# Attention and Strassen's FFN1 on one core: a planner by due times, block 0's sums shared by VectorE and GpSimd, first maxima on TensorE, every other block backward

## The chip, the core and the metric

The kernel runs on one core of a Trainium2 chip. The metric is the device time of one execution in microseconds. TensorE (PE), VectorE (DVE), ScalarE (ACT), GpSimd (POOL) and SyncE (SP, which issues DMAs) each run their own instructions in the order in which the program lists them, and wait for one another by semaphores.

## What is computed

Linear attention over 8 batches, 8 heads, 576 positions of 64, and then a feed-forward network on the 4608 x 512 result. The weights are float64, the rest float32.

```python
q_s = softmax(q, over the 64 of a head)
k_s = softmax(k, over the 576 positions)      # needs a maximum over positions
kv  = einsum('bhsd,bhde...', k_s^T, v)        # 64 x 64 for each head
x   = (q_s @ kv), reshaped to 4608 x 512
h   = x @ w_in                                # 512 x 2048
g   = h * sigmoid(1.702 h)
out = g @ w_out                               # 2048 x 512
```

## The kernel before

**Blocks, pairs, steps.** The 4608 tokens are nine blocks of 512. FFN1 and FFN2 of a block take eight steps, one for each *pair* p of w_in's and w_out's column groups. A step has 15 slots. In it `ffn1` does Strassen's seven products (line 581), each as six matmuls of 256 columns, in two PSUM banks, Y and Z (`PROD`, line 561). VectorE's adds (line 594) and ScalarE's copies empty these banks, and the same bank is written again by the next product but one. `ffn2` (line 643) follows one step later in banks 0 to 3. The last step's sums are copied out (line 655) and stored.

**Splits.** A product is made of float32r halves: a value's rounded part h (a cast on ScalarE) and its remainder l = value - h (a subtraction: line 551 for x, 625 for g, 274 for w_in, 312 for w_out). Strassen's sums come before that: s1, s2, s3, s4 of x in `x_sums` (line 525; VectorE in block 0, GpSimd in the others), and four sums of w_in's parts (line 251, GpSimd) in the staging tile `st`.

**Weights.** w_in and w_out come as float64 and are turned into float32 on the chip while block 0 runs: `high` (line 238, ScalarE, on the upper words), `low` (242, VectorE, shifts the lower words), `narrow` (234 and 235, two VectorE instructions: the first joins the words, the second puts the sign back). `conv_wi` then makes the seven tiles `wa` (3) and `wb` (4) of a pair, and stores them to DRAM (`kept`, line 277). There are two buffers each of `wa` and `wb` (p % 2), so in blocks 1 to 8 `load_kept` (line 288) brings each pair back, by DMAs that GpSimd issues. The w_out tiles stay.

**Attention.** The attention of block t runs beside the FFN of block t - 1 (block 0's own at the start). Key batch b belongs to block t = b; I call it key block b. `k_max` has VectorE take maxima over the 4 positions of a partition (lines 382 to 384), and GpSimd the maximum over the 128 partitions, for each of four head pairs (`partition_all_reduce`, line 388). `k_sub` subtracts it (400, 403) and ScalarE takes exp (406). `q_soft` (460 to 470) does the same for q along a row, `q_tr` transposes q on PE (483), `kv_pairs` (437) and `x_pairs` (504) are the small matmuls. ScalarE needs one table for exp and one for gelu (597).

**The order.** Every operation is given to `Plan` with an engine, a cost, what it reads and writes, and a rank. `Plan.order` (line 47) plays the engines forward: whenever one is free it takes, of its ready operations, the one with the lowest rank. The order in which the operations began is the program's order on every engine. The costs are those of lines 24 and 99 to 108; a change of ScalarE's table costs 1.28 us there, one of GpSimd's programs nothing.

```python
def dve(n, psum=False):
    return 0.15 + n / 960
...
def pool(n):
    return 0.25 + n / 480
```

The functions that the change touches, and what calls them:

Of the kernel before, what the change touches and what calls it, by code (L numbers as in the profile page):

```python
# [18 lines left out]
class Plan:  # L19
# [4 lines left out]
    HOP, LAND, RATE, ISSUE, TABLE = 0.1, 1.8, 270e3, 0.5, 1.28  # L24
# [22 lines left out]
    def order(self):  # L47
        ops = self.ops
        left = [len(o[2]) for o in ops]
        users = [[] for _ in ops]  # L50
        for n, o in enumerate(ops):
            for d in o[2]:
                users[d].append(n)
        engines = sorted({o[0] for o in ops})
        free = dict.fromkeys(engines, 0.0)
        ready = {e: [] for e in engines}
        coming = []
        at = [0.0] * len(ops)
        for n, o in enumerate(ops):
            if not left[n]:  # L60
                heapq.heappush(ready[o[0]], (o[3], n))
        wire, table = 0.0, None
        began = []
        self.start = {}
        now = 0.0
        while len(began) < len(ops):
            while coming and coming[0][0] <= now:
                _, n = heapq.heappop(coming)
                heapq.heappush(ready[ops[n][0]], (ops[n][3], n))
            moved = False  # L70
            for e in engines:
                if free[e] > now or not ready[e]:
# [10 lines left out]
                self.start[n] = now  # L83
                moved = True
                for u in users[n]:
# [5 lines left out]
            if not moved:  # L91
                times = [f for e, f in free.items() if f > now and ready[e]]
                if coming:
                    times.append(coming[0][0])
                now = min(t for t in times if t > now) if any(t > now for t in times) else now
        return began


def dve(n, psum=False):
# [7 lines left out]
def pool(n):  # L107
    return 0.25 + n / 480
# [3 lines left out]
def efficient_attention_then_gelu_ffn(  # L112
# [54 lines left out]

    ident = sb("ident", [P, P])
# [9 lines left out]
    st = sb("st", [P, 7, 2 * P])  # L178
# [4 lines left out]
    mx = [sb(f"mx{i}", [P, 2, D]) for i in range(2)]  # L183
    m1 = sb("m1", [P, 2, 2, D])
    qm = [sb(f"qm{i}", [P, 2 * C]) for i in range(2)]
# [9 lines left out]
    first = sb("first", [P, D])  # L195
    nc.vector.memset(first, 0.0)
    nc.gpsimd.partition_all_reduce(first, first, P, bass_isa.ReduceOp.max)
# [5 lines left out]
    plan.add("POOL", 7.0, (), ("first",), -3000, lambda: None)  # L203
# [8 lines left out]
    def load_w(p, kind, rank):  # L212
        for jj in range(2):
# [12 lines left out]
            plan.add("SP", plan.ISSUE, (), (tag,), rank + 0.01 * jj, run, size=2 * DM * 4 * P)  # L226

    def words(raw):
        return raw.rearrange("p (f t) -> p f t", t=2)

    def narrow(f, w):
# [16 lines left out]
    ST_ = [("st", n) for n in range(7)]  # L248

    def sub(o, x, y):  # L250
        nc.gpsimd.tensor_tensor(out=st[:, o], in0=st[:, x], in1=st[:, y], op=ALU.subtract)

    def conv_wi(p, rank):
        i = p % 2
        for jj, at_ in enumerate((0, 5)):
            T, K = f"wo{p}{jj}", ST_[at_ : at_ + 2]
            f = flat(st[:, at_ : at_ + 2])
# [6 lines left out]
            plan.add("DVE", 1.36, (T, *K), K, rank, lambda f=f, w=w: narrow(f, w()))  # L264
# [477 lines left out]
```

## Time and profile before

| | us |
|---|---|
| median of 3 runs | 1035.72 (1033.41 to 1045.96) |
| the profiled execution | 1033.14 |
| its span in the profile | 1031.4 |
| PE busy | 865.9 (84%) |
| VectorE busy | 567.9 (55%) |
| ScalarE busy | 498.3 (48%) |
| GpSimd busy | 207.0 (20%) |

The span runs from the first to the last instruction of the program. "Idle before" in a row is how long the engine did nothing just before the instruction, with the event that ended it.  Granted clock 1.00 is 2.4 GHz for TensorE, 0.50 is 1.2 GHz.

### The profile page before, as it was taken

The page shows a single profiled execution, that of the slowest core. Times are in us where ns is not written, and L with a number is a line of the kernel's source. Part 1 is how long each engine was busy: PE and PEld are TensorE (multiplying, and loading weights), DVE is VectorE, ACT ScalarE, POOL GpSimd, SP SyncE. Part 2 cuts the span into 40 slices and gives each one's busy share as a digit, 9 for nine tenths or more (in the row PEclk, how much of TensorE's full clock was granted, in tenths as well). Part 3 has the DMA queues.
Part 4 walks back from the last instruction along what each step waited for, and adds up shares of the span by engine and source line. Part 5 has one row for each costly group of instructions (what it writes and reads, how often), then busy time and mean ns, then how long its engine had stood idle before and what let it go on. Part 6 is the DMA issues. An engine that isn't in the chain of part 4 may idle for free.

```text
span 1031.4 us, 15064 instructions
## 1 busy us (share of the span) xinstructions
PE 865.9 (84%) x5792; PEld 748.3 (73%) x5792; DVE 567.9 (55%) x1103; ACT 498.3 (48%) x861; POOL 207.0 (20%) x247
## 2 busy tenths in 40 slices
PE   3523873457689999999796999997999999999998
PEld 2322652346568898888686789886889889888887
DVE  7885994549677343453565653535553663235332
ACT  3552753347658343543555942526543742334322
POOL 1432332323232011120133021101311211021100
PEclk9675996669899999999998999998999999999999
DMA  9991842149565565466757655566476556447551
GB/s 256 277 328 46 246 147 91 49 152 253 177 171 177 184 215 171 136 235 202 209 152 208 205 179 173 182 229 177 131 235 204 173 173 219 150 143 237 164 181 42
DMA packets 126088, 187.64 MB, mean 182 GB/s; under 512 B 84544, under 2 KB 100928, under 8 KB 116800
## 3 DMA queue, kind: packets, MB, share of 16 engines
q0 software_dynamic: 18432, 117.45, 34.9%
q1 hardware_dynamic: 107584, 69.22, 23.0%
q8 instruction: 46, 0.75, 0.3%
q14 instruction: 26, 0.21, 0.1%
HBM read 162.53 MB, written 24.12 MB: 181 GB/s over the span
## 4 chain that ended last, share of the span: by engine, by line
PE 66%; DVE 14%; issue 7%; DMA 5%; ACT 2%; SPq 2%; POOL 2%; DVEq 0%; POOLq 0%; ACTq 0%
PE bank L643 32%; PE bank L581 30%; DMA qt<-in_q 2%; PE bank L504 2%; DVE gl L625 1%; DMA kt<-in_k 1%; PE bank L437 1%; PE bank L483 1%; DVE qt L461 1%; DVE xl L551 1%; SPq L368 1%; DVE kt L400 1%; DVE raw L242 1%; DMA vt<-in_v 1%; DVE g L594 1%
## 5 line engine op out<-in xcount | busy, mean ns | idle before, releaser
L643 PE MATMUL bank<-w,gh 128*128 128x512 f32 x1152 | 372.8, 405 | 34.8 <-ACT w L308 26.3
L581 PE MATMUL bank<-xh,wb 128*128 128x256 f32 x1152 | 257.0, 288 | 30.5 <-DVE tu L594 13.3
L643 PE MATMUL bank<-w,gl 128*128 128x512 f32 x576 | 230.4, 400 | 11.2 <-DVE gl L625 11.2
L581 PE MATMUL bank<-xh,wa 128*128 128x256 f32 x864 | 190.1, 294 | 56.0 <-POOL wa L274 20.7
L643 PEld LDWEIGHTS bank<-w,gh 128*128 128x128 f32 x1152 | 194.1, 193 | 57.3 <-ACT w L308 27.1
L581 PEld LDWEIGHTS bank<-xh,wb 128*128 128x128 f32 x1152 | 199.1, 192 | 49.1 <-DVE tu L594 15.7
L581 PEld LDWEIGHTS bank<-xh,wa 128*128 128x128 f32 x864 | 149.6, 197 | 71.4 <-POOL wa L274 21.9
L581 PE MATMUL bank<-xl,wb 128*128 128x256 f32 x576 | 164.6, 286 | 0.0
L597 ACT ACTIVATE g<-g 128x512 f32<-128x512 f32 (+1 forms) x144 | 75.5, 525 | 176.2 <-DVE g L594 171.4
L643 PEld LDWEIGHTS bank<-w,gl 128*128 128x128 f32 x576 | 110.6, 192 | 42.5 <-DVE gl L625 15.8
L625 DVE TENSOR_TENSOR gl<-g,gh 128x512 fp32r<-128x512 f32 x144 | 110.1, 772 | 28.2 <-ACT gh L622 27.9
L581 PE MATMUL bank<-xl,wa 128*128 128x256 f32 x432 | 125.4, 290 | 0.0
L581 PEld LDWEIGHTS bank<-xl,wb 128*128 128x128 f32 x576 | 110.4, 192 | 9.6
L594 DVE TENSOR_TENSOR tu<-bank,ta 128x256 f32<-128x256 f32 x72 | 30.4, 422 | 134.2 <-PE bank L581 134.2
L622 ACT CAST gh<-g 128x512 fp32r<-128x512 f32 x144 | 89.4, 621 | 4.5
L288 POOL DMA_DIRECT2D wb<-kb x64 | 35.4, 552 | 275.8 <-PE bank L581 275.8
L581 PEld LDWEIGHTS bank<-xl,wa 128*128 128x128 f32 x432 | 85.3, 197 | 5.0
L288 POOL DMA_DIRECT2D wa<-ka x64 | 35.2, 550 | 259.7 <-PE bank L581 242.6
L597 ACT ACTIVATE g<-bank 128x256 f32<-128x256 f32 x72 | 27.7, 385 | 71.0 <-PE bank L581 70.0
L400 DVE TENSOR_TENSOR kt<-kt,mx 128x512 f32<-128x512 f32 x32 | 24.9, 779 | 61.4 <-POOL mx L388 61.4
L594 DVE TENSOR_TENSOR g<-bank,ts 128x256 f32<-128x256 f32 x72 | 30.4, 422 | 46.3 <-PE bank L581 45.7
L594 DVE TENSOR_TENSOR g<-bank,ta 128x256 f32<-128x256 f32 x72 | 30.5, 423 | 46.0 <-PE bank L581 45.6
(76 smaller groups left out, 968.1 us busy)
## 6 DMA issues: line engine op xcount, KB each, us to landing
wb<-kb POOLq DMA_DIRECT2D x64, 1024.0 KB, 5.2
wa<-ka POOLq DMA_DIRECT2D x64, 768.0 KB, 4.7
out<-tmp SPq DMA_DIRECT2D x36, 256.0 KB, 4.2
kt<-in_k SPq DMA_DIRECT2D x32, 256.0 KB, 3.9
vt<-in_v SPq DMA_DIRECT2D x64, 128.0 KB, 4.1
raw<-in_moe_w_in SPq DMA_DIRECT2D x16, 512.0 KB, 8.7
raw<-in_moe_w_out SPq DMA_DIRECT2D x16, 512.0 KB, 4.8
kb<-wb SPq DMA_DIRECT2D x8, 1024.0 KB, 5.1
```

What stands on the lines that cost most here:

```text
L242: nc.vector.tensor_scalar(lo, lo, 29, None, ALU.logical_shift_right)
L288: nc.gpsimd.dma_start(out=tl.rearrange("p s n f -> p (s n f)"), in_=kept[p][u == "wb"])
L368: nc.sync.dma_start(out=qt[hp][p0:p1, :, o : o + m], in_=src.rearrange("h (p c) d -> p c h d", c=C))
L400: nc.vector.tensor_tensor(out=t, in0=t, in1=m.unsqueeze(2).broadcast_to([P, 2, CM, D]), op=ALU.subtract)
L437: nc.tensor.matmul(pk[r0 : r0 + D, m, :], lhs, rhs, start=c == 0, stop=c == CM, tile_position=(0, r0))
L504: nc.tensor.matmul(po[ro], kvn[b % 2][ri, hp, :], qx[ri], start=True, stop=True, tile_position=((a ^ odd) * D, a * D),)
L581: nc.tensor.matmul(ph[bk], tl[:, s, place, c * P : (c + 1) * P], x[:, c, :], start=opens and c == 0 and e == 0, stop=c == 1 and e == 2, sk ...
L594: return lambda: nc.vector.tensor_tensor(out=o, in0=ph[bk], in1=x, op=ALU.add)
L597: return lambda: nc.scalar.activation(o, x, AF.Gelu_apprx_sigmoid)
L622: vec("ACT", act(2 * n), half, (H,), slot, lambda c=c, gh=gh: nc.scalar.copy(gh, c))
L625: nc.vector.tensor_tensor(out=gl, in0=c, in1=gh.bitcast(F32), op=ALU.subtract)
L643: nc.tensor.matmul(bank[c], l, r, start=first_ and e == 0, stop=last and e == 2)
```

## The change

- **Due times.** `Plan.due` walks backward from the PE operations, which are laid end to end in rank order, and gives each operation the latest time at which it may begin. `Plan.forward` takes the ready operation with the earliest due time instead of the lowest rank. SP may be at most 6 us of transfer ahead of the wire. A change of GpSimd's program costs 7.0 us there now, and the DMA rate is 310 GB/s instead of 270.
- **Shared operations.** An operation of the kind `EITHER` goes to VectorE or GpSimd, whichever is free first. `sb_op` makes such an operation; its callers ask for it in block 0 and for the attention of block 1: the sums of w_in's parts, the remainders of `wa`, `wb`, w_out, x and g, `k_sub`, the subtraction and the scaling of `q_soft`, `x_sums`. Otherwise `sb_op` puts it on VectorE. So `x_sums` of blocks 2 to 8 moves from GpSimd to VectorE.
- **First maxima.** For key blocks 0 and 1 the maximum over partitions is a transpose on PE, a reduction on VectorE, a matmul of the broadcast column with the identity, and a copy on ScalarE. From key block 2 on it is the all-reduce, which reads the tokens of all shared operations added so far (`summed`). The first all-reduce, on the tile `first`, is gone, and `ident` is made first.
- **narrow** is one instruction: `high` uses Prelu with a negative slope of -2^32 in place of a copy, which leaves the sign where the shift needs it.
- **Order of pairs.** Odd blocks take the pairs from 7 to 0. The first two steps of blocks 1 to 8 find their pair still in `wa` and `wb`, so `load_kept` leaves those out: 48 loads each of `wa` and `wb` instead of 64.
- **Staging.** `st` becomes two buffers, by the parity of p; the second lies in the space of pair 7's weights, whose w_in load waits for the buffer's last use. `mx` has four buffers instead of two.

The core of the diff:

```diff
-    HOP, LAND, RATE, ISSUE, TABLE = 0.1, 1.8, 270e3, 0.5, 1.28
+
+
+
+
+    HOP, LAND, RATE, ISSUE = 0.1, 1.8, 310e3, 0.5
+    AHEAD = 6.0
+    TABLE = {"ACT": 1.28, "POOL": 7.0}
+    EITHER = ("DVE", "POOL")
...
+    def due(self):
+        ops = self.ops
+        at = [float("inf")] * len(ops)
+        time = 0.0
+        for n in sorted((n for n, o in enumerate(ops) if o[0] == "PE"), key=lambda n: (ops[n][3], n)):
+            at[n] = time
+            time += ops[n][1]
+        for n in reversed(range(len(ops))):
+            for d in ops[n][2]:
+                e, cost, _, _, _, _, size = ops[d]
+                cost = cost[0] if e is self.EITHER else cost
+                need = cost + self.HOP + (size / self.RATE + self.LAND if size else 0.0)
+                at[d] = min(at[d], at[n] - need)
+        return at
...
+                mine = [ready[e]] + ([ready[self.EITHER]] if e in self.EITHER else [])
+                mine = [r for r in mine if r]
+                if free[e] > now or not mine:
                     continue
-                _, n = heapq.heappop(ready[e])
-                _, cost, _, _, _, needs, size = ops[n]
-                if needs is not None and needs != table:
-                    cost, table = cost + self.TABLE, needs
+                _, n = heapq.heappop(min(mine))
+                kind, cost, _, _, _, needs, size = ops[n]
+                if kind is self.EITHER:
+                    self.taken[n] = e
+                    cost, needs = (cost[0], None) if e == "DVE" else (cost[1], needs)
...
+                    if e == "SP":
+                        free[e] = max(free[e], wire - self.AHEAD)
...
+    def sb_op(shared, n, reads, writes, rank, run):
+
+        if shared:
+            plan.add(
+                plan.EITHER, (dve(n), pool(n)), reads, (*writes, sums()), rank, lambda e: run(engines[e]), table="sum"
+            )
+        else:
+            plan.add("DVE", dve(n), reads, writes, rank, lambda: run(nc.vector))
...
+            held = [("st", 1, jj, m) for m in range(3 + jj)] if p == SPARE and kind == "wi" else []
+            plan.add("SP", plan.ISSUE, (), (tag, *held), rank + 0.01 * jj, run, size=2 * DM * 4 * P)
...
+    def high(f, w):
+
+        nc.scalar.activation(f, w[:, :, 1].bitcast(F32), AF.Prelu, scale=2.0**-112, alpha=-(2.0**32))
...
         nc.vector.scalar_tensor_tensor(fi, fi, 3, w[:, :, 0], ALU.logical_shift_left, ALU.bitwise_or)
-        nc.vector.scalar_tensor_tensor(fi, w[:, :, 1], -0x80000000, fi, ALU.bitwise_and, ALU.bitwise_or)
-
-    def high(f, w):
-        nc.scalar.activation(f, w[:, :, 1].bitcast(F32), AF.Copy, scale=2.0**-112)
...
+    def pair(t, step):
+
+
+        return NS - 1 - step if t % 2 else step
+
+    def load_kept(t, step):
+        if step < 2:
+            return
+        p = pair(t, step)
...
+        if b > 1:
+            plan.add("POOL", 0.92, (M, *summed), (M,), rank, reduce, table="max")
+            return
+
+        bk = next_bank(b)
+        pb, col = bank[bk], cols[s % 2]
+        PB, CK = ("bank", bk), ("col", s % 2)
+        flat_m = m.rearrange("p h d -> p (h d)")
+
+        def run_c():
+            nc.vector.tensor_reduce(out=col, in_=pb[:, 0:P], axis=AX.X, op=ALU.max)
+
+        def run_b():
+            nc.tensor.matmul(pb[:, P : 2 * P], col.broadcast_to([P, P]), ident, start=True, stop=True)
+
+        plan.add("PE", 0.15, (M, "ident"), (PB,), rank, lambda: nc.tensor.transpose(pb[:, 0:P], flat_m, ident))
+        plan.add("DVE", dve(P), (PB,), (CK,), rank, run_c)
+        plan.add("PE", 0.25, (CK, "ident"), (PB,), rank, run_b)
+        plan.add("ACT", act(P), (PB,), (M,), rank, lambda: nc.scalar.copy(flat_m, pb[:, P : 2 * P]))
...
-        E = nc.vector if t == 0 else nc.gpsimd
-        name, cost = ("DVE", dve(2 * HT)) if t == 0 else ("POOL", pool(2 * HT))
...
+            sb_op(t < 2, 2 * HT, r, (w,), rank, run)
...
+            sb_op(t == 0, 2 * n, (*half, H), (L,), R(t, step, slot) - PRIOR, run_l)
...
+        r = R(0, SPARE - 2, -19.95) if p == SPARE else -900 + p
+        at(r, lambda rank, p=p: load_w(p, "wi", rank))
```

## Rows read from the trace of the kernel before

**Rows 1.** The page's part 2: busy tenths of PE in 40 equal slices of the span (25.8 us each), and under them TensorE's granted clock in tenths of full speed.
```profile
PE   3523873457689999999796999997999999999998
...
PEclk9675996669899999999998999998999999999999
```
**Rows 2.** The timeline (start us, us, engine line op out<-in xcount, idle time before and what ended it): the first product of FFN1, and the first output copy of block 0.
```profile
38.40 0.58 PE L581 MATMUL bank<-xh,wa 128*128 128x256 f32 x1 [5.99 <-ACT wa L279]
...
262.97 0.57 ACT L655 COPY tmp<-bank 128x512 f32<-128x512 f32 x1
```
**Rows 3.** Busy time by stretch, each from one block's first output copy to the next one's (from: to, length, then for PE, PEld, DVE, ACT and POOL the busy us and the instructions in brackets, then the granted clock, DMA's share and GB/s). The first row begins at the first product.
```profile
38.40:262.97 224.57, 125.55 (x796) 102.12 (x797) 161.51 (x270) 113.95 (x182) 73.89 (x62) 0.77 0.53 166
262.97:370.75 107.78, 92.64 (x618) 78.91 (x617) 66.62 (x140) 63.79 (x109) 22.54 (x27) 0.94 0.60 179
370.75:457.40 86.65, 86.65 (x554) 77.21 (x553) 39.30 (x77) 37.86 (x67) 13.71 (x20) 1.00 0.57 188
457.40:572.84 115.44, 101.47 (x775) 88.65 (x774) 62.43 (x137) 61.65 (x108) 24.67 (x29) 0.96 0.65 194
572.84:660.54 87.70, 85.73 (x541) 75.43 (x540) 45.43 (x85) 45.81 (x78) 13.19 (x19) 1.00 0.58 184
660.54:762.22 101.68, 96.29 (x738) 85.11 (x737) 53.40 (x113) 51.18 (x93) 17.52 (x24) 0.97 0.62 190
...
851.24:939.79 88.55, 88.55 (x562) 77.83 (x561) 33.45 (x65) 33.62 (x65) 13.57 (x20) 1.00 0.54 178
```
**Rows 4.** The waits of PE from 38.4 to 262.97 us (engine line <- what it waited for: us in total, times, longest us).
```profile
PE bank L643 <- ACT w L308: 26.3, 2, 23.8
PE bank L581 <- POOL wa L274: 20.7, 5, 15.2
PE bank L581 <- ACT wa L279: 14.6, 3, 6.0
PE bank L581 <- POOL wb L274: 10.8, 1, 10.8
...
PE bank L581 <- DVE ts L594: 2.9, 2, 1.7
PE bank L581 <- DVE tu L594: 2.5, 3, 1.6
...
PE bank L581 <- DVE g L594: 1.8, 2, 1.3
```
**Rows 5.** GpSimd: two rows of its timeline in block 0, and a row of the waits of the whole span ("issue": it waited for nothing that the profile shows).
```profile
72.87 1.43 POOL L388 PARTITION_ALL_REDUCE mx<-mx  x2 [7.45 <-issue]
...
215.41 1.79 POOL L274 TENSOR_TENSOR wa<-st,wa 128x768 fp32r<-128x768 f32 x1 [7.12 <-issue]
...
POOL mx L388 <- issue: 69.7, 8, 10.9
```
**Rows 6.** The timeline from 530 to 560 us: GpSimd, and VectorE's instruction that waits for it.
```profile
551.32 1.43 POOL L388 PARTITION_ALL_REDUCE mx<-mx  x2 [10.85 <-issue]
552.63 0.74 POOL L288 DMA_DIRECT2D wb<-kb  x1
554.68 1.80 POOL L388 PARTITION_ALL_REDUCE mx<-mx  x1 [1.32 <-DVE mx L384]
...
552.08 0.92 DVE L400 TENSOR_TENSOR kt<-kt,mx 128x512 f32<-128x512 f32 x1 [9.43 <-POOL mx L388]
```
**Rows 7.** Groups of instructions of VectorE by line and shape, whole span (busy us, mean ns | idle time before them).
```profile
L594 DVE TENSOR_TENSOR tu<-bank,ta 128x256 f32<-128x256 f32 x72 | 30.4, 422 | 134.2 <-PE bank L581 134.2
...
L234 DVE SCALAR_TENSOR_TENSOR tmp<-tmp,raw 128x512 int32<-128x512 int32 x16 | 11.2, 700 | 1.1
...
L383 DVE TENSOR_TENSOR mx<-m 128x128 f32<-128x128 f32 x32 | 9.7, 305 | 1.1
```
**Rows 8.** The timeline again: single instructions of VectorE and GpSimd, alone (3.75, 25.20, 38.09, 912.31) and beside one another (the others).
```profile
3.75 0.42 DVE L382 TENSOR_TENSOR m<-kt 128x256 f32<-128x256 f32 x1 [1.43 <-DMA kt<-in_k]
...
25.20 0.42 DVE L242 TENSOR_SCALAR raw<-raw 128x512 uint32<-128x512 uint32 x1
...
38.09 0.68 DVE L551 TENSOR_TENSOR xl<-xa,xh 128x512 fp32r<-128x512 f32 x1
38.69 2.29 DVE L551 TENSOR_TENSOR xl<-s,xh 128x512 fp32r<-128x512 f32 x1
...
38.42 2.01 POOL L274 TENSOR_TENSOR wa<-st,wa 128x768 fp32r<-128x768 f32 x1 [3.22 <-ACT wa L279]
...
101.03 0.68 DVE L467 TENSOR_REDUCE qm<-qt 128x8 f32<-128x512 f32 x1
101.74 1.66 DVE L468 TENSOR_SCALAR qm<-qm 128x8 f32<-128x8 f32 x1
...
100.48 2.90 POOL L274 TENSOR_TENSOR wb<-st,wb 128x1024 fp32r<-128x1024 f32 x1 [1.78 <-issue]
...
912.31 1.30 POOL L525 TENSOR_TENSOR xa<-xa 128x512 f32<-128x512 f32 x1
```
**Rows 9.** Busy time from 20 to 40 us (columns as in rows 3), and the DMA view from the start to 262.97 us.
```profile
20.00:40.00 20.00, 9.75 (x70) 4.35 (x70) 17.44 (x33) 12.18 (x23) 5.59 (x6) 0.77 1.10 350
...
DMA packets 54030, 48.15 MB, mean 183 GB/s; under 512 B 37120, under 2 KB 49408, under 8 KB 52864
```
**Rows 10.** ScalarE's table loads in front of the gelus of line 597 (busy us, mean ns).
```profile
L597 ACT ACT_TABLE_LOAD x40 | 51.3, 1283 | 0.7
```

More of the change, by code (lines that the diff above doesn't have):

```diff
@@ L60, in order @@
             if not left[n]:
[L61 to L64, printed above, removed]
+                heapq.heappush(ready[o[0]], (due[n], n))
+        wire, table = 0.0, {"POOL": "sum"}
+        began, start, end = [], [0.0] * len(ops), 0.0
+        self.taken = {}
         now = 0.0
@@ L81, in order @@
                     done = wire + self.LAND
+                    if e == "SP":
+                        free[e] = max(free[e], wire - self.AHEAD)
                 began.append(n)
-                self.start[n] = now
-                moved = True
-                for u in users[n]:
+                start[n] = now
+                end = max(end, done)
+                for u in self.users[n]:
                     left[u] -= 1
@@ L90, in order, with emit, dve @@
                         heapq.heappush(coming, (at[u], u))
[L91 to L95, printed above, removed]
-        return began
-def dve(n, psum=False):
+            times = [f for e, f in free.items() if f > now and (ready[e] or e in self.EITHER and ready[self.EITHER])]
+            if coming:
+                times.append(max(coming[0][0], now))
+            if times:
+                now = min(times)
+        return began, start, end
+    def order(self):
+        self.users = [[] for _ in self.ops]
+        for n, o in enumerate(self.ops):
+            for d in o[2]:
+                self.users[d].append(n)
+        began, self.start, self.end = self.forward(self.due())
+        return began
+    def emit(self):
+        for n in self.order():
+            run = self.ops[n][4]
+            if n in self.taken:
+                run(self.taken[n])
+            else:
+                run()
+def dve(n):
     return 0.15 + n / 960
@@ L107, in pool @@
 def pool(n):
-    return 0.25 + n / 480
+    return 0.25 + n / 440
 @with_exitstack
@@ L202, in efficient_attention_then_gelu_ffn @@
         nc.vector.memset(t[:, :, :, D:W], 1.0)
-    plan.add("POOL", 7.0, (), ("first",), -3000, lambda: None)
+    plan.add("POOL", 0.7, (), ("ident",), -3000, lambda: None)
     def R(t, step, off=0.0):
@@ L288, in run @@
                 nc.gpsimd.dma_start(out=tl.rearrange("p s n f -> p (s n f)"), in_=kept[p][u == "wb"])
-            plan.add("POOL", 1.0, ((u, "kept", p),), ((u, i),), R(t, p - 2, off), run, size=n * 4 * P * P * 4)
+            plan.add("POOL", 1.0, ((u, "kept", p),), ((u, i),), R(t, step - 2, off), run, size=n * 4 * P * P * 4)
     nt = [0]
@@ L564, in efficient_attention_then_gelu_ffn, with ffn1 @@
     }
-    def ffn1(t, p):
-        i = gi = p % 2
+    def ffn1(t, step):
+        i, gi = pair(t, step) % 2, step % 2
         ca, cb = gt[0][gi], gt[1][0]
@@ L587, in product @@
             PB = ("bank", bk)
-            plan.add("PE", 0.71, reads if opens else [*reads, PB], (PB,), R(t, p, OPS[n][2]), run)
+            plan.add("PE", 0.71, reads if opens else [*reads, PB], (PB,), R(t, step, OPS[n][2]), run)
         def vec(engine, cost, reads, writes, slot, run, table=None):
-            plan.add(engine, cost, reads, writes, R(t, p, slot) - PRIOR, run, table=table)
+            plan.add(engine, cost, reads, writes, R(t, step, slot) - PRIOR, run, table=table)
         def plus(o, bk, x):
@@ L622, in ffn1, with run_l, ffn2 @@
             vec("ACT", act(2 * n), half, (H,), slot, lambda c=c, gh=gh: nc.scalar.copy(gh, c))
-            def run_l(c=c, gh=gh, gl=gl):
-                nc.vector.tensor_tensor(out=gl, in0=c, in1=gh.bitcast(F32), op=ALU.subtract)
-            vec("DVE", dve(2 * n), (*half, H), (L,), slot, run_l)
-    def ffn2(t, p):
-        gi = p % 2
+            def run_l(E, c=c, gh=gh, gl=gl):
+                E.tensor_tensor(out=gl, in0=c, in1=gh.bitcast(F32), op=ALU.subtract)
+            sb_op(t == 0, 2 * n, (*half, H), (L,), R(t, step, slot) - PRIOR, run_l)
+    def ffn2(t, step):
+        p, gi = pair(t, step), step % 2
         ov = out[t * TB : (t + 1) * TB, :].rearrange("(p c) m -> p c m", c=C)
@@ L636, in ffn2 @@
             for jj in range(2):
-                first_, last = p == 0 and jj == 0, p == NS - 1 and jj == 1
+                first_, last = step == 0 and jj == 0, step == NS - 1 and jj == 1
                 def run(c=c, jj=jj, x=x, cs=cs, first_=first_, last=last):
@@ L715, in efficient_attention_then_gelu_ffn @@
     with tc.manual_schedule():
-        for n in plan.order():
-            plan.ops[n][4]()
+        plan.emit()
 _INS = ["q", "k", "v", "moe_w_in", "moe_w_out"]
```

138 lines of the change are left out of this document (71 added, 67 removed).

## The prediction

> **What bounds the kernel now.** I read the page's slices first [rows 1]. They tell two stories: PE at 2 to 8 tenths, with the granted clock down to 5 tenths, in most of the first dozen, and 9 tenths at full clock in most of the others. So I cut the span at each block's first output copy (line 655) [rows 2] and read busy time between those marks [rows 3]. A block whose PE never waits takes 88.55 us (851.24 to 939.79, PE busy all of it). From the first product at 38.40 [rows 2] to the first mark at 262.97, block 0 takes 224.57 with PE busy 125.55 at a clock of 0.77. The next block takes 107.78, and two later ones 115.44 and 101.68. Everything to be won lies in block 0 (some 135 us), block 1 (19) and those two (27 and 13); the rest is at PE's own speed.
>
> The waits of block 0 [rows 4] put PE behind the w_in and w_out splits: 26.3 us for a cast of w, 20.7 and 10.8 for GpSimd's subtraction, 14.6 for a cast of wa. These lead back to GpSimd [rows 5]: whenever it passes between the partition all-reduce of the key maxima (388) and a tensor_tensor (251, 274, 525) it is idle for some 7 us, mostly for nothing that the profile shows. I call that a reload. The timeline has twelve between 60 us and the first mark, at 72.87 the first and at 215.41 the last. The later losses have the same look: in the stretch of 115.44, GpSimd is idle 10.85 us before an all-reduce, VectorE's kt subtraction waits 9.43 us for it, and PE for the PSUM add queued behind that [rows 6].
>
> **Reloads.** For key blocks 0 and 1 the maxima go over TensorE, and from key block 2 every all-reduce reads a token of all GpSimd sums that were planned before; later sums go to VectorE. One reload is left, in block 1, and the planner now charges 7.0 us for it. The replacement costs, for each of 8 pairs, two small PE instructions and, on as many columns as line 383 has, a reduction on VectorE and a copy on ScalarE. Line 383 takes 0.31 [rows 7]; at that price for each of the four (an estimate) it is 5 us on PE and 2.5 on VectorE and ScalarE each, spread out, against 8 all-reduces. I set it at nothing on PE, whose waits in block 0 are many times that; if that cover goes it costs its 5 us.
>
> **VectorE and GpSimd share block 0.** Here I expect less than the planner does, since it lets both run freely. At 38.69 the subtraction of line 551 takes 2.29 us, against 0.68 just before, and ends 0.55 after GpSimd's subtraction, which ran from 38.42 for 2.01: it began when that was over [rows 8]. The tensor_scalar of line 468, on 8 columns, takes 1.66, to the end of GpSimd's 2.90. The reduction of line 467 beside the same instruction keeps its 0.68. So one of the two is let in at a time, unless VectorE has a single ordinary SBUF input.
>
> The Trainium skill, "SBUF — State Buffer", section "Who interferes with whom", states this as an exclusive lock on a shared port pair, held for the whole instruction, and speaks against the sharing; the rows agree. With the lock the sum below is 169 us, without it 120.
>
> The sum for everything up to the first mark, in VectorE's undisturbed durations [rows 7, 8]:
> - Holds the pair, VectorE only: 32 shifts of line 242 at 0.42; 32 at 0.69 for narrow (64 before, since Prelu now carries the sign); k_max 8 x (0.42 + 2 x 0.28; line 383's mean has some blocked ones in it). 13.4 + 22.1 + 7.8 = 43.3.
> - Holds it and may go to either: 32 stage subtractions at 0.42; 8 wa and 8 wb remainders at 0.96 and 1.23 (estimates: 0.42 at 256 and 0.69 at 512 columns, carried on); 32 at 0.69 for w and g remainders; k_sub 8 x 0.96; 16 of q at 0.69; 8 sums at 0.68; 14 xl at 0.69. Together 86.8, 134 instructions.
> - Without the pair: 40 PSUM adds at 0.42, 16 reductions at 0.67, small ones: 34.
> GpSimd takes 1.30 for 512 columns where VectorE takes 0.68, a ratio of 1.9. With half shared out, the pair is held 43.3 + 43.4 + 1.9 x 43.4 = 169 us, and the 34 fit under GpSimd's 82. With all on VectorE it is 43.3 + 86.8 + 34 = 164; with three quarters on GpSimd, 189. Sharing is worth nothing either way, and the pair is the bound. I take half, as both queues have work throughout.
>
> The same count for before: VectorE 43.3, the 53.2 of the shared work that it did, 22.1 for the second narrow, and 13.2 because three blocks' keys and q are done by the mark instead of two, together 132; GpSimd 1.9 x 33.6 for the other shared work, 64. That is 196, and the first max starts at 3.75, so 262.97 - 3.75 - 196 = 63 us were neither; twelve reloads of about 7 us, some beside VectorE's work, fill that. For after I leave 13 of the 63 for ordinary hand-overs. First mark: 3.75 + 169 + 13 = 186, so -77. Bounds: PE alone, start (38.40 - 2) + 88.55 + 3 (FFN2's first copy comes at slot 3 of 15 of the next step) = 128; all 63 left: 236. DMA doesn't lift the lower bound: 48 MB had moved by the mark, 5 of them weights read back, and 43 MB at the 350 GB/s of 20 to 40 us [rows 9] are 123 us.
>
> **The rest.** Start: narrow saves 2 x 0.69 and the first maxima come a little sooner; 2 us, already inside the 186. Block 1: 107.78 to 91 (88.55 and a little for the last reload), -17; bounds -19 and 0. The blocks of 115.44 and 101.68 go to 88.6: -27 and -13; bounds 0 and this. The others (86.65 and 87.70 among them) may give back 3 in all, as work no longer runs ahead. x_sums on VectorE: 4 x 0.68 = 2.7 us per block, where it is busy 33.45 of 88.55 [rows 3]; nothing, and at worst 2.7 x 7 = 19. Backward order drops 16 of the 64 loads of kept wa and as many of wb; no wait of PE names them [rows 4], so nothing, or 3 us at block 1's beginning. The second stage buffer takes waits away from ScalarE, which isn't the bound: nothing. In exchange pair 7's w_in loads wait for that buffer's last use; pair 7 comes last and its 1 MB is 3 us at the rate above, so two steps cover it; if not, 3. Due times and SP's six-microsecond lead reorder the queues; I take zero for it, inside the bounds of 128 and 236.
>
> Sum: -77 - 17 - 27 - 13 + 3 = -131. The profiled execution took 1033.14 for a span of 1031.4; the span becomes 900, the time **902 us**. The runs' median of 1035.72 stands 2.6 above that execution, within their spread.
>
> **Rivals.**
> - *The sharing works*: the pair is held less, PE sets block 0, the first mark is near 132, time 848. For it: VectorE is idle in places where GpSimd could run alone. Against: the row of 2.29 us. 14%.
> - *The change doesn't do what it says*: GpSimd still reloads, since its DMA issues or the identity mask change programs too, or the one reload left stalls PE and the later losses stay: +40, 942. Against: at 554.68 an all-reduce follows the DMA issue of 552.63 after 1.32 us of waiting for VectorE alone [rows 6]. 10%.
> - *Prelu needs its own table.* Each table load takes 1.283 us [rows 10]; no row shows a Prelu. If 32 of them each bring one and a reload for exp or gelu, ScalarE has 64 x 1.283 = 82 us more in front of the mark: 186 + 82, time 984. 6%. The Trainium skill, "ScalarE: Activation LUTs", section "Table sets: the hidden batching unit", says that cheap functions stand in every set and names relu, copy, identity, abs, not Prelu; it counts a switch with its drain as 2.66 us, by which the price would be 170.
> - *Slower: GpSimd's instructions land on PE's chain.* In block 0 PE has two banks, Y and Z, and each waits for a VectorE add. If an add stands behind a VectorE instruction that GpSimd blocks, PE pays GpSimd's 1.23 (82.5 us over 67 instructions) and the 0.69 of the blocked one. With 67 that is 129 us and the kernel is where it was; above 68 it is slower; with three quarters on GpSimd (100, the pair held 189) the mark is near 398 and the time 1114. Against: in block 0 of before PE waits only 2.9 + 2.5 + 1.8 us for these adds [rows 4] with 52 such instructions. 6%, the half of it within 2%.
>
> **How the numbers follow.** 64% for the forecast (870 to 940). The range 850 to 965 takes in most of the first rival, the second, and the mark's bound of 236 (952); about 15% lie outside. Two per cent is what a measurement of this kernel tells from no change. Faster by over 2%: 0.93. Within: 0.03. Slower: 0.04, one hundredth of it for what I haven't thought of.
>
> **What would show it.** GpSimd's unexplained idle time: one instance near 7 us after block 0, instead of the eight before all-reduces alone [rows 5]. First mark near 186, then every block 87 to 92. In block 0, VectorE's two-input instructions beside a GpSimd tensor_tensor at 1.3 to 3 us, its PSUM adds at 0.42; PE still with gaps and spells of half clock. No table load in front of a Prelu. I am wrong if the mark lies below 150 (no lock, or little given to GpSimd), if it lies above 230, or if a later block again takes over 100.

## The result, and the profile after

The kernel after takes **922.63 us** (median; 1034.57 for the kernel before beside it), a ratio of **0.890, 95% interval 0.884 to 0.897**; 902 was forecast, in a range of 850 to 965. Measured again beside the experiments it took 920.1 (918.29 to 926.27), ratio 0.887 [0.884, 0.890]. One execution, with every matmul at some 2.7 times its usual length (2887.71 us), is left out of these numbers, and as it was the profiled one, the profile shown here is that of the second measurement, with a span of 916.5 us.

The page's parts 1 and 2, kernel after (columns as in [rows 1]; a slice is 22.9 us):

```profile
PE 852.7 (93%) x5816; PEld 740.6 (81%) x5816; DVE 558.6 (61%) x1079; ACT 499.3 (54%) x871; POOL 181.4 (20%) x205
...
PE   4477786899999999999999999999999999999998
...
PEclk9789999799999999999999999999999999999999
```

PE is at 9 tenths from the ninth slice on, where [rows 1] still had sixes and sevens up to the twenty-eighth. TensorE's clock dips to 7 tenths twice, where it went down to 5. The two marks of [rows 2], timeline of the kernel after:

```profile
31.40 0.38 PE L678 MATMUL bank<-xh,wa 128*128 128x256 f32 x1 [2.00 <-ACT wa L343]
...
180.07 0.59 ACT L752 COPY tmp<-bank 128x512 f32<-128x512 f32 x1 [4.52 <-PE bank L740]
```

The start is 7.0 us shorter, the first mark 82.9 us earlier. Busy time by stretch, kernel after, as in [rows 3] (PE, PEld, VectorE, ScalarE, GpSimd, clock, DMA, GB/s); the last two rows are everything up to the first mark and everything behind it:

```profile
31.40:180.07 148.67, 111.70 (x667) 91.71 (x668) 137.64 (x194) 90.33 (x159) 90.84 (x66) 0.88 0.71 225
180.07:276.33 96.26, 95.01 (x743) 83.91 (x743) 72.45 (x163) 77.35 (x123) 19.14 (x24) 1.00 0.70 197
276.33:369.44 93.11, 91.53 (x654) 80.82 (x653) 59.25 (x129) 63.04 (x106) 10.97 (x16) 1.00 0.56 164
...
457.83:553.84 96.01, 95.01 (x738) 82.98 (x737) 55.58 (x124) 50.41 (x94) 11.21 (x18) 1.00 0.64 187
...
644.36:735.87 91.51, 91.51 (x658) 80.80 (x657) 47.33 (x95) 47.14 (x81) 6.35 (x12) 1.00 0.46 144
735.87:824.70 88.83, 88.83 (x562) 77.80 (x561) 35.96 (x69) 33.60 (x66) 6.33 (x12) 1.00 0.43 137
...
0.00:180.07 180.07, 125.52 (x791) 100.30 (x792) 162.40 (x249) 105.37 (x191) 106.08 (x85) 0.90 0.75 229
...
180.07:916.50 736.43, 727.15 (x5027) 640.31 (x5026) 396.19 (x830) 393.94 (x680) 75.32 (x120) 1.00 0.52 159
```

The same two cuts of the kernel before:

```profile
0.00:262.97 262.97, 138.44 (x908) 109.16 (x909) 191.37 (x339) 131.98 (x217) 81.57 (x77) 0.79 0.60 183
...
262.97:1031.40 768.43, 727.46 (x4886) 639.18 (x4884) 376.55 (x765) 366.35 (x645) 125.47 (x171) 0.98 0.58 182
```

These four rows hold the whole difference. Of 114.9 us of span, 82.9 lie ahead of the first mark: VectorE's idle time there goes from 262.97 - 191.37 = 71.6 to 180.07 - 162.40 = 17.7 (53.9 us), and its busy time falls by 29.0. The other 32.0 lie behind it. There PE is busy as long as before (727.46 and 727.15 us), and its idle time falls from 41.0 to 9.3.

The waits of PE between the two marks, to be read against [rows 4]:

```profile
PE bank L479 <- DVE mx L456: 11.1, 4, 3.6
PE bank L740 <- DVE w L384: 6.7, 2, 3.4
PE bank L678 <- DVE g L691: 5.5, 4, 2.5
PE bank L740 <- DVE gl L722: 4.5, 4, 1.5
PE bank L678 <- DVE wa L338: 2.7, 3, 1.4
PE bank L678 <- DVE ts L691: 2.2, 2, 1.6
```

The waits of 10 to 26 us for GpSimd and the casts are gone. The largest is new: for 11.1 us the transposes of key block 1's maxima (line 479) wait for VectorE's part of these maxima (line 456). GpSimd's waits of the whole span that end without a cause in the profile ([rows 5] had 69.7 us in eight before the all-reduces alone):

```profile
POOL ident masks.py:199 <- issue: 7.0, 1, 7.0
...
POOL mx L460 <- issue: 6.0, 1, 6.0
...
POOL wb L360 <- issue: 4.3, 1, 4.3
```

And where they lie, in GpSimd's timeline:

```profile
7.91 0.28 POOL masks.py:199 TENSOR_SCALAR_AFFINE_SELECT ident<-ident 128x128 f32<-128x128 f32 x1 [6.98 <-issue]
...
173.53 1.29 POOL L722 TENSOR_TENSOR gl<-g,gh 128x512 fp32r<-128x512 f32 x1 [0.76 <-ACT gh L719]
...
180.78 0.72 POOL L460 PARTITION_ALL_REDUCE mx<-mx  x1 [5.96 <-issue]
```

The reload of 5.96 us is the one forecast, behind the last sum. The one of 6.98 us was not: the identity matrix is made first, its affine_select waits for a reload, and PE's first instruction starts at 8.25, when that is done. The Trainium skill, "GPSIMD Engine Reference", section "2.1 Instruction dispatch", has the first call to a freshly loaded kernel pay some 6 us that no instruction shows; the traces here agree (5.96 and 6.98 us above), and show it again each time the programs alternate (5.8 to 8.1 us for the twelve in block 0 of the kernel before).

### The profile page after: what moved, and what is told of

The parts are those of the page before. It is cut to its first block, busy times and chain, and to the rows that moved or that the text cites. A ratio compares the mean times of both kernels' runs of the same rounds, so it can differ in the third digit from the quotient of the medians.

```text
span 2885.9 us, 14967 instructions
## 1 busy us (share of the span) xinstructions
PE 2861.8 (99%) x5816; PEld 2113.2 (73%) x5816; DVE 539.7 (19%) x1079; ACT 503.9 (17%) x871; POOL 167.6 (6%) x205
## 4 chain that ended last, share of the span: by engine, by line
PE 99%; DVE 1%; DMA 0%; issue 0%; ACT 0%; SPq 0%; POOL 0%; POOLq 0%
PE bank L740 49%; PE bank L678 43%; PE bank L529 2%; PE bank L581 2%; PE bank L602 2%; PE bank L477 0%; DVE m L454 0%; DMA ka<-wa 0%; DMA qt<-in_q 0%; DVE mx L455 0%; DVE mx L456 0%; DVE wb L338 0%; PE bank L479 0%; DVE wa L338 0%; POOL qt L566 0%
## 5 line engine op out<-in xcount | busy, mean ns | idle before, releaser
L740 PE MATMUL bank<-w,gh 128*128 128x512 f32 x1152 | 1108.4, 1096 | 0.0
L678 PE MATMUL bank<-xh,wb 128*128 128x256 f32 x1152 | 707.5, 686 | 1.6 <-DVE ts L691 0.6
L740 PEld LDWEIGHTS bank<-w,gh 128*128 128x128 f32 x1152 | 519.2, 486 | 153.9 <-issue 150.4
L740 PE MATMUL bank<-w,gl 128*128 128x512 f32 x576 | 626.4, 1088 | 0.0
L678 PEld LDWEIGHTS bank<-xh,wb 128*128 128x128 f32 x1152 | 510.4, 458 | 115.0 <-issue 89.7
L678 PE MATMUL bank<-xh,wa 128*128 128x256 f32 x864 | 513.4, 682 | 0.5 <-ACT ta L702 0.5
L678 PEld LDWEIGHTS bank<-xh,wa 128*128 128x128 f32 x864 | 392.4, 476 | 72.4 <-issue 64.4
L678 PE MATMUL bank<-xl,wb 128*128 128x256 f32 x576 | 392.0, 681 | 0.0
L678 PEld LDWEIGHTS bank<-xl,wb 128*128 128x128 f32 x576 | 268.1, 465 | 97.5 <-issue 96.7
L678 PE MATMUL bank<-xl,wa 128*128 128x256 f32 x432 | 292.0, 676 | 0.0
L722 DVE TENSOR_TENSOR gl<-g,gh 128x512 fp32r<-128x512 f32 x138 | 95.6, 699 | 24.3 <-ACT gh L719 23.7
L360 POOL DMA_DIRECT2D wa<-ka x48 | 25.8, 537 | 1231.1 <-PE bank L678 1231.1
```

The source lines that it names most:

```text
L360: nc.gpsimd.dma_start(out=tl.rearrange("p s n f -> p (s n f)"), in_=kept[p][u == "wb"])
L678: nc.tensor.matmul(ph[bk], tl[:, s, place, c * P : (c + 1) * P], x[:, c, :], start=opens and c == 0 and e == 0, stop=c == 1 and e == 2, sk ...
L722: E.tensor_tensor(out=gl, in0=c, in1=gh.bitcast(F32), op=ALU.subtract)
L740: nc.tensor.matmul(bank[c], l, r, start=first_ and e == 0, stop=last and e == 2)
```

## The experiments

Twelve kernels ran, each against the kernel before. Times are medians; the mark, and VectorE's busy and idle time up to it, are from each one's profile.

| kernel | us (lowest to highest) | ratio to before [95%] | first mark | VectorE busy / idle to it |
|---|---|---|---|---|
| before (beside them) | 1038.05 to 1040.17 | 1 | 263.0 | 191.4 / 71.6 |
| after_again | 920.1 (918.3-926.3) | 0.887 [0.884, 0.890] | 180.1 | 162.4 / 17.7 |
| no_share | 901.0 (899.3-903.3) | 0.868 [0.866, 0.870] | 157.7 | 141.6 / 16.1 |
| idle_sums | 934.9 (929.8-936.3) | 0.900 [0.897, 0.903] | 180.4 | 165.6 / 14.7 |
| idle_memsets | 905.0 (901.6-907.8) | 0.871 [0.868, 0.875] | 157.5 | 142.7 / 14.9 |
| all_reduce | 915.4 (914.8-917.3) | 0.882 [0.880, 0.884] | 174.6 | 154.3 / 20.4 |
| all_reduce_uncharged | 1013.2 (1010.8-1018.0) | 0.974 [0.970, 0.979] | 264.5 | 149.9 / 114.7 |
| before_on_vector | 933.9 (932.8-938.6) | 0.898 [0.894, 0.903] | 200.1 | 175.8 / 24.3 |
| no_share_reduce_1 | 896.7 (893.7-898.2) | 0.864 [0.861, 0.866] | 160.8 | 141.3 / 19.5 |
| no_share_reduce_all | 891.9 (888.8-892.8) | 0.859 [0.856, 0.862] | 155.3 | 141.0 / 14.3 |
| two_narrow | 944.4 (942.6-945.7) | 0.909 [0.907, 0.911] | 202.8 | 184.8 / 18.0 |
| rank_order | 934.2 (931.5-936.6) | 0.898 [0.893, 0.902] | 187.2 | 163.8 / 23.4 |
| forward_pairs | 916.1 (915.7-924.1) | 0.883 [0.877, 0.889] | 177.2 | 160.0 / 17.2 |

**after_again.** The kernel after, unedited.

> The changed kernel once more, for a trace at the ordinary clock. Forecast's theory (the pair of VectorE and GpSimd bounds block 0, the rest runs at PE's speed): about 922 us as timed, first mark near 206, blocks after it 87 to 92, one idle stretch of GpSimd near 7 us for nothing shown. Rival (block 0 is as short as the planner thinks and a later block loses): first mark below 150 and a later stretch above 100.

It took 920.1; its profile is the one above. The rival is out: no stretch behind the mark takes over 100 us. But the mark near 206 that I gave the forecast's theory, to make up the 922 us, is wrong too: it lies at 180.1, and the blocks behind it take up to 96.3 us.

**no_share.** No operation is shared: VectorE has all of them.

```diff
-        if shared:
+        if False:
```

> Every operation that the change lets either engine take goes to VectorE; GpSimd is left with the identity, the all-reduces from key block 2 on, and DMA issues. Pair theory: VectorE's sum to the first mark is 164 us where the shared split holds the pair 169, so the time moves less than 15 us either way (907 to 937). Rival (GpSimd's work runs beside VectorE's): VectorE has 164 instead of 120 us to do, time some 40 us longer, 962.

901.0, below the 907 to 937 that I expected: the sharing that the change brings **costs 19 us**. Up to the mark VectorE is busy 141.62 us with 310 instructions, where the kernel after has 162.40 with 249:

```profile
0.00:157.69 157.69, 122.70 (x789) 98.78 (x790) 141.62 (x310) 104.41 (x191) 0.68 (x6) 0.89 0.83 265
```

The same VectorE instructions in the two kernels say why. Groups by line and shape up to the mark, kernel after (busy, mean ns | idle before):

```profile
L297 DVE TENSOR_SCALAR raw<-raw 128x512 uint32<-128x512 uint32 x32 | 19.2, 609 | 0.0
...
L722 DVE TENSOR_TENSOR gl<-g,gh 128x512 fp32r<-128x512 f32 x10 | 12.2, 1217 | 0.0
...
L691 DVE TENSOR_TENSOR tu<-bank,ta 128x256 f32<-128x256 f32 x8 | 3.4, 422 | 5.9 <-PE bank L678 5.9
```

and no_share:

```profile
L297 DVE TENSOR_SCALAR raw<-raw 128x512 uint32<-128x512 uint32 x32 | 13.0, 418 | 0.1
...
L722 DVE TENSOR_TENSOR gl<-g,gh 128x512 fp32r<-128x512 f32 x15 | 10.2, 681 | 0.5 <-ACT gh L719 0.5
...
L691 DVE TENSOR_TENSOR tu<-bank,ta 128x256 f32<-128x256 f32 x8 | 3.3, 416 | 0.3 <-PE bank L678 0.3
```

A subtraction of two SBUF tiles takes 1.22 us on average in the kernel with GpSimd's sums and 0.68 in the one without; a shift 0.61 and 0.42; an add with one input in PSUM stays at 0.42. That fits the lock of the prediction, but GpSimd's sums also carry results that others wait for.

**idle_sums and idle_memsets.** To have GpSimd's presence alone, both begin from no_share and give GpSimd work whose results nobody reads, behind each of the 16 remainders of wa and wb (and `mx` has two buffers, for space). The first adds five subtractions of 128 x 256 that read SBUF, 75.9 us in 80 instructions; the second ten memsets of the same size that only write it, 53.7 us in 160, behind one subtraction of a single column. The diff is that of idle_sums; in idle_memsets `nc.gpsimd.memset(scr, 0.0)`, twice, stands for the subtraction, and the first of the five has the subtraction of one column in front of it.

```diff
+            for _ in range(5):
+
+                def run_x(x=flat(tl[:, 0]).bitcast(F32)[:, 0 : 2 * P]):
+                    nc.gpsimd.tensor_tensor(out=scr, in0=x, in1=x, op=ALU.subtract)
+
+                plan.add("POOL", pool(2 * P), (*K, (u, i)), ("scr",), rank, run_x, table="sum")
```

> no_share (all on VectorE, 901 us), with mx in two buffers to make room, and 80 subtractions of 128x256 on GpSimd whose result nobody reads: five after each wa and wb remainder of block 0, some 0.73 us each, 58 us in all, reading wa or wb. Pair theory: VectorE's two-input instructions wait for each of them; VectorE is in such instructions for most of block 0, so 25 to 45 us more, 926 to 946, and its instructions of 0.68 us take 1.2 and more beside them. Rival (GpSimd's work costs only through where the planner puts it, not by being there): within 6 us of 901.

> As idle_sums, but 160 memsets of 128x256 on GpSimd in the same places (behind one subtraction of a single column for each wa and wb, which only sets the time), so GpSimd is about as busy but reads nothing. Pair theory: a GpSimd instruction that reads nothing leaves VectorE's reads alone, within 6 us of 901. Rival (any GpSimd instruction slows VectorE, or what hurts is the semaphores and the order): as much as idle_sums.

The sums cost 34 us against no_share, the memsets 4 (the ranges of the runs overlap). Of the 30.4 us between the profiled spans of idle_sums and no_share, 22.7 lie ahead of the mark, where VectorE is busy for 24.0 us longer and idle no longer than in no_share; the rest lies behind it and is not explained. Groups of VectorE up to the mark in idle_sums:

```profile
L298 DVE TENSOR_SCALAR raw<-raw 128x512 uint32<-128x512 uint32 x32 | 18.7, 598 | 0.0
...
L729 DVE TENSOR_TENSOR gl<-g,gh 128x512 fp32r<-128x512 f32 x15 | 12.4, 824 | 0.0
```

and in idle_memsets:

```profile
L298 DVE TENSOR_SCALAR raw<-raw 128x512 uint32<-128x512 uint32 x32 | 14.1, 455 | 0.0
...
L732 DVE TENSOR_TENSOR gl<-g,gh 128x512 fp32r<-128x512 f32 x15 | 10.2, 682 | 0.0
```

Among memsets the subtraction keeps its 0.68; among sums that nobody needs it takes 0.82 on average. That mean is a mixture, as the timeline of idle_sums shows for one that runs behind GpSimd's sums and one that runs beside them (I had expected 1.2 and more for the latter):

```profile
97.69 0.68 DVE L729 TENSOR_TENSOR gl<-g,gh 128x512 fp32r<-128x512 f32 x1
...
103.78 1.10 DVE L729 TENSOR_TENSOR gl<-g,gh 128x512 fp32r<-128x512 f32 x1
...
91.35 4.93 POOL L349 TENSOR_TENSOR scr<-wa 128x256 f32<-128x256 f32 x5 [5.47 <-ACT wa L344]
102.74 1.59 POOL L349 TENSOR_TENSOR scr<-wb 128x256 f32<-128x256 f32 x1 [6.46 <-ACT wb L344]
```

So it is what GpSimd reads, not its results, that slows VectorE's subtractions. The Trainium skill, "SBUF — State Buffer", section "Who interferes with whom", states just this: two SBUF inputs on VectorE contend with a GpSimd instruction that reads SBUF, not with one that only writes it. These two runs agree.

**all_reduce and all_reduce_uncharged.** The first sends the maxima of key blocks 0 and 1 to GpSimd again, wherever the planner wants them; the second also takes away the planner's price for a change of GpSimd's program (the last two lines).

```diff
-        if b > 1:
-            plan.add("POOL", 0.92, (M, *summed), (M,), rank, reduce, table="max")
+        if True:
+            plan.add("POOL", 0.92, (M,), (M,), rank, reduce, table="max")
...
-    TABLE = {"ACT": 1.28, "POOL": 7.0}
+    TABLE = {"ACT": 1.28, "POOL": 0.0}
```

> The maxima over partitions of key blocks 0 and 1 by GpSimd's all-reduce again, without the tokens that hold the later ones back; sharing and all else as changed. Reload theory: in block 0 GpSimd passes between its two programs at least four times at some 7 us each, and VectorE and PE wait behind some of them: 20 to 60 us more, 942 to 982, with idle stretches of GpSimd of 6 to 8 us for nothing shown. Rival (the reloads were hidden, the order of the queues was what mattered): under 8 us more.

> As all_reduce, but the planner charges nothing for a change of GpSimd's program. all_reduce took 915 with some ten reloads before its first mark, fewer than half of GpSimd's sums, and VectorE idle only 20 us. Theory A (reloads cost when the order doesn't know of them, as in the kernel before): more changes of program, VectorE waits behind them, 15 to 50 us over all_reduce. Theory B (reloads cost little in any order, what was won came from elsewhere): within 8 us of 915.

With the price: 915.4. Without: 1013.2, almost the kernel before, from one number in a table. The rows up to the mark, all_reduce first, and GpSimd's unexplained waits in all_reduce_uncharged:

```profile
0.00:174.65 174.65, 119.29 (x764) 97.69 (x765) 154.26 (x278) 106.10 (x186) 64.16 (x55) 0.89 0.77 240
...
0.00:264.55 264.55, 129.38 (x774) 105.40 (x775) 149.88 (x255) 112.61 (x193) 98.63 (x87) 0.82 0.51 158
```

```profile
POOL mx L460 <- issue: 36.2, 6, 6.5
...
POOL kt L489 <- issue: 25.0, 3, 10.7
```

VectorE is idle for 114.7 us of it, in all_reduce for 20.4. So the order that doesn't know the reload's price pays it, by VectorE standing still, and by more than the 15 to 50 us that I expected. For all_reduce the reload theory missed: it forecast 20 to 60 us more than the kernel after, and the kernel is 5 us faster, although GpSimd changes its program ten times up to the mark (16 times without the price). VectorE is idle there for only 2.7 us longer than in the kernel after: it is not the number of reloads that costs, but what waits behind them. Moving the maxima to TensorE was thus not needed to avoid the loss; an order planned with the 7 us is enough. What the ten reloads or the maxima on TensorE cost can't be read from all_reduce against the kernel after, since the planner also gave GpSimd fewer sums there (55 us of them up to the mark, against 107).

**before_on_vector.** The kernel before with the three kinds of GpSimd sums (lines 251, 274, 525) on VectorE, at VectorE's cost in the plan; nothing else of the change.

```diff
-        nc.gpsimd.tensor_tensor(out=st[:, o], in0=st[:, x], in1=st[:, y], op=ALU.subtract)
+        nc.vector.tensor_tensor(out=st[:, o], in0=st[:, x], in1=st[:, y], op=ALU.subtract)
...
-                nc.gpsimd.tensor_tensor(out=tl[:, 1], in0=f, in1=tl[:, 0].bitcast(F32), op=ALU.subtract)
+                nc.vector.tensor_tensor(out=tl[:, 1], in0=f, in1=tl[:, 0].bitcast(F32), op=ALU.subtract)
...
-        E = nc.vector if t == 0 else nc.gpsimd
+        E = nc.vector
```

> The kernel before with all of GpSimd's subtractions and sums (lines 251, 274, 525) on VectorE, with VectorE's costs; order by rank, two-instruction narrow, one staging tile and all else as before. GpSimd then has one program, so no reloads, and nothing that holds the pair. Theory (reloads and the pair were block 0's loss): VectorE has about 142 + 22 + some 13 us of work for a third key block, with 20 idle, first mark near 197 and later stretches 87 to 97, about 930. Rival (the order and the staging were the loss): VectorE's idle time stays above 50, time above 970.

933.9, as expected: three lines give 104 of the 118 us. Up to the mark VectorE's idle time falls from 71.6 to 24.3, and its busy time too, from 191.4 to 175.8, though it has taken over GpSimd's sums: its two-input instructions take less (line 625 0.69 us instead of 1.00 on average), and the earlier mark has less of the next key blocks' work in front of it (9 of the subtractions of line 400 instead of 12). The edit takes away the reloads and GpSimd's reads beside VectorE together, so this run doesn't part the two.

**no_share_reduce_1 and no_share_reduce_all.** On no_share, the maxima of key block 1, then of blocks 0 and 1 (`if True:`), go to GpSimd.

```diff
-        if b > 1:
+        if b > 0:
```

> no_share with the all-reduce from key block 1 on instead of 2: GpSimd has no sums, so nothing to reload for. VectorE loses four reductions (1.2 us), PE and ScalarE four small instructions each. Theory: 898 to 901, no more than 3 us. Rival (the all-reduce's longer way holds up VectorE or its load hits the DMA issues): 3 to 8 us slower.

> no_share with the all-reduce for every key block, as before the change: what the first maxima on TensorE are worth by themselves. In all_reduce the first product came at 38.8 instead of 31.4 us, since GpSimd loads a program for the identity and another for the all-reduce. Theory: the start is 6 to 7 us later, and block 0, which VectorE bounds, gives back 2 of them: 905 to 908. Rival (VectorE's other work fills the wait): within 2 us of 901.

896.7 and 891.9, against 901.0, both below what I expected: on no_share, the **maxima on TensorE cost 9 us**. I expected a later start for the second; it is not later (first product at 30.46, in no_share 31.83), since there PE's first transpose has to wait as well, until 8.85, for the identity and the reload in front of it, and the first subtraction of line 489 begins at 16.07, here at 15.81. The rows up to the mark and behind it, no_share first:

```profile
0.00:157.69 157.69, 122.70 (x789) 98.78 (x790) 141.62 (x310) 104.41 (x191) 0.68 (x6) 0.89 0.83 265
157.69:901.60 743.91, 730.27 (x5029) 641.20 (x5027) 402.87 (x850) 383.85 (x674) 74.03 (x120) 1.00 0.51 157
...
0.00:155.33 155.33, 116.58 (x765) 94.03 (x766) 141.00 (x302) 103.05 (x182) 12.86 (x14) 0.93 0.86 269
155.33:890.30 734.97, 726.76 (x5029) 640.27 (x5027) 402.71 (x850) 389.09 (x678) 74.04 (x120) 1.00 0.52 158
```

Of the 11 us between the two spans 2.4 lie ahead of the mark and 8.9 behind it, though all of the TensorE maxima run ahead of it. Ahead of it PE is busy for 6.1 us less, with their 24 instructions gone. Behind it PE has the same 5029 instructions, is busy for 3.5 us less and waits 5.4 us less; why, I have not isolated. **no_share_reduce_all beats both kernels**: 28 us below after, ratio 0.859 to before.

**two_narrow.** `high` copies, without Prelu, and `narrow` has its second instruction again.

```diff
-        nc.scalar.activation(f, w[:, :, 1].bitcast(F32), AF.Prelu, scale=2.0**-112, alpha=-(2.0**32))
+        nc.scalar.activation(f, w[:, :, 1].bitcast(F32), AF.Copy, scale=2.0**-112)
...
+        nc.vector.scalar_tensor_tensor(fi, w[:, :, 1], -0x80000000, fi, ALU.bitwise_and, ALU.bitwise_or)
```

> narrow in two VectorE instructions again, high a plain copy instead of Prelu; all else as changed. Pair theory (VectorE with GpSimd is the bound of block 0): 32 x 0.69 = 22 us more, 944. Rival (PE, ScalarE or DMA bounds block 0): under 6 us more, 922 to 928. If Prelu loads tables, fewer table loads than in the changed kernel.

944.4, 24 us more; VectorE's 32 more instructions are 22.4 us of busy time, as the one term of 22.1 in the sum had it.

**rank_order.** The plan goes by rank again instead of by due times.

```diff
-        began, self.start, self.end = self.forward(self.due())
+        began, self.start, self.end = self.forward([o[3] for o in self.ops])
```

> The changed kernel with the old ranks in the place of due times in the forward play; charges, shared operations and all else as changed. What the runs so far show: VectorE is busy 162 of the 180 us to the first mark, so the order can at most cost what VectorE would then idle. Theory (what was won is VectorE's work and its waits for reloads, not the order): within 10 us of the changed kernel's 920. Rival (due times won most of block 0): VectorE's idle time goes from 18 back towards the 71 of before, 20 to 50 us more.

934.2, 14 us more, between what the two theories gave: 7.1 ahead of the mark (VectorE idle 23.4 instead of 17.7, first product 36.2 instead of 31.4) and 6 behind it.

**forward_pairs.** Every block goes forward, and all pairs are loaded again.

```diff
-        return NS - 1 - step if t % 2 else step
+        return step
...
-        if step < 2:
-            return
```

> All blocks take the pairs from 0 to 7, and every step of blocks 1 to 8 loads its pair again (64 loads each of wa and wb instead of 48); all else as changed. Forecast's theory: no wait of PE hangs on these loads, under 3 us. Rival (block 1 waits for its first pair's load while the DMA queues are full of block 0's stores): 5 to 15 us more, at the beginning of block 1.

916.1, with an interval that overlaps that of the kernel after: the backward order is worth nothing that these runs can tell.

## Why the prediction came out as it did

The change is 20 us slower than forecast (922.6 against 902), for which two terms account, one on each side of the mark: of the span (916.5 for 900), 22.4 us too little behind it and 5.9 too much ahead of it.

- **Behind the mark: the step that was mis-sized.** I forecast 900 - 186 = 714 us, from "a block whose PE never waits takes 88.55". Measured are 736.4. The stretch of 88.55 holds 562 PE instructions and no matmul of a key block (line 437); in the kernel after, stretches with 738 or 743, among them those of two key blocks (160 of line 529), need 95.0 us of PE. The rows were at hand: [rows 3] has PE *busy* for 101.47, 96.29 and 92.64 us in the three stretches that I cut to 88.6, 88.6 and 91. PE is busy for 727.5 us behind the mark of before, and for 722 to 734 us in every kernel measured here; 714 lies below all of them. The sign "then every block 87 to 92" failed too: three of the eight stretches behind the mark take 93.1 to 96.3 us. "The others may give back 3 in all, as work no longer runs ahead" is the same error: block 0 of before ran 908 PE instructions by the mark, after 791, so the blocks behind it took on 141 (4886 to 5027), at a clock of 1.00 instead of 0.98. Of the 41.0 us of idle PE time, 31.7 were won. The mechanism held: the two reload stalls in 115.44 and 101.68 are gone.
- **Up to the mark: 180.1 for 186, close by luck, since two errors cancel.** The half share was low: GpSimd took 79 of the shared instructions, 49.3 of the 86.8 us at the sum's own prices, 57%. With that my sum gives 43.3 + 37.5 + 1.9 x 49.3 = 174 us of the pair held against 164 with all on VectorE, 10 apart; measured are 22.4 between the marks and 19 between the times. So "sharing is worth nothing either way" fails: the direction follows from the rule, some half of the size does not, and where it comes from is open. (GpSimd's own records of the 79 add up to 107 us, for 94 in the sum: they too are longer beside VectorE's, line 722 1.60 us on average instead of 1.30.) The other way, durations of neighbouring records overlap, and a sum of them is too long: in no_share VectorE's 310 records add up to 160.2 us, close to the 164, and cover 141.6; in the kernel after 249 add up to 175.7 and cover 162.4. In the kernel after:

```profile
67.85 0.41 DVE L691 TENSOR_TENSOR g<-bank,tu 128x256 f32<-128x256 f32 x1
68.18 1.45 DVE L293 SCALAR_TENSOR_TENSOR tmp<-tmp,raw 128x512 int32<-128x512 int32 x1
69.56 2.03 DVE L338 TENSOR_TENSOR wa<-st,wa 128x768 fp32r<-128x768 f32 x1
...
67.60 5.12 POOL L489 TENSOR_TENSOR kt<-kt,mx 128x512 f32<-128x512 f32 x3
```

  The second begins 0.08 us before the first ends. The rows also show what was forecast: a PSUM add at 0.41 and two-input instructions at 1.45 (0.69 alone) and 2.03 (0.95 in no_share, 0.96 as estimated) beside three subtractions of GpSimd.
- **Reloads: right.** One after block 0, and the twelve of block 0 gone; 13 us of VectorE's idle time were left for hand-overs besides 3.75 at the start, measured 17.7 in all. What was missed is the one in front of the identity, and that ten of them, planned for, leave VectorE idle for no more than 20.4 us in all_reduce.
- **First maxima: cost set at nothing, 9 us measured (on no_share).** I set it at nothing because PE's waits in block 0 were many times longer; those went away (the largest is now the 11.1 us in front of line 479), and with them the cover that I named. The 6.1 us of PE busy time is near the 5 us that I estimated for that case; but only 2.4 of the profile's 11 us lie in that stage, and the rest is not explained.
- **Due times at zero: 14 us.** The bounds held it; zero, without a reason for it, was too low.
- **narrow: right** (22.1 of 24). **Prelu: right**, no table load ahead of one (82 loads in the span against 80 before, 8 against 22 up to the mark). **Backward order: right**, nothing.
- **The rivals.** That sharing works fell with no_share. That GpSimd's instructions land on PE's chain fell with the waits: 5.5 + 2.2 + 0.5 = 8.2 us for VectorE's adds, where before had 7.2 and the rival 129. That GpSimd still reloads came true only in front of the identity, and Prelu brought no table of its own.

The parts, measured one at a time on the kernel after, are: one narrow -24, due times -14, sharing +19, first maxima +9 (this on no_share). Together they are -10, and before_on_vector at 933.9 less 10 is close to the 920.1 of the whole. The second staging buffer, SP's lead and the planner's other prices (the DMA rate, and pool(n), which became 0.25 + n/440) were not measured by themselves. So nearly all of the gain (104 of the 118 us) is what before_on_vector brings: no reloads that VectorE stands behind, and no reads of GpSimd beside VectorE's. The pair of all_reduce kernels, with sums on GpSimd in both, gives 98 us to the order around the reloads, which speaks for them as the larger part; how the 104 us divide between the two is not measured.

## What to carry to other kernels

Before a block is given a best case, add up the busy time of the engine that will bound it, stretch by stretch: here no stretch went below its own. When an engine pays for changing its program, put that price into whatever orders the work, and look in the trace for who waits behind each change: the time appears as idle time of other engines and under no instruction, and their number alone doesn't tell it. Handing VectorE's two-input sums to GpSimd is no gain where VectorE bounds the stage: each holds the other up, and here the kernel is faster with GpSimd all but idle.

## What the runs showed of the hardware that had not been expected

- A reload of 7.0 us stands in front of the first affine_select too, and delays PE's first work to 8.25 us. It doesn't where an all-reduce came before: in the kernel before and in before_on_vector the same instruction starts at 12.24 and 11.63 us, less than 0.1 us behind its memset.
- Memsets on GpSimd leave VectorE's two-input subtraction at 0.68 us, and lengthen a shift a little, from 0.418 to 0.455 on average; sums lengthen it to 0.6.
- One DMA issue of GpSimd's, at 186.62 us between the first all-reduces of the kernel after, waits 4.3 us for nothing that the profile shows; what it waits for is open.
